# The first key chunk of an adaLN block: key rows in eight loads, the modulation in finer pieces between the key matmuls

## The chip, the cores and the metric

One core of a Trainium2 chip runs the program. The metric is device microseconds (us) of one execution. Five engines matter: TensorE (PE, with its weight loads as PEld), VectorE (DVE), ScalarE (ACT), GpSimd (POOL) and SyncE (SP, which issues nearly all transfers).

## The reference, cut to what matters

```python
x = A_x                                            # 2048 x 1024, bf16
mod = (silu(c) @ w_mod).reshape(1, 6, 1, -1)       # sa, ca, ga, sb, cb, gb: 1024 each
h = layernorm(x) * (1 + ca) + sa
q, k, v = split(h @ wqkv)                          # 32 heads of 32
pq, pk = phi(q), phi(k)                            # where(t > 0, t + 1, exp(t)) + 1e-6
o = (pq @ sum(pk v)) / (pq @ sum(pk) + 1e-6)       # linear attention
x = x + ga * (o @ wo)
h = layernorm(x) * (1 + cb) + sb
out = x + gb * ((silu(h @ w_gate) * (h @ w_up)) @ w_down)
```

## The kernel before, in words

The 2048 rows are cut in four chunks of 512, each of four tiles of 128 rows. A chunk's `hT` holds the layer-normed and modulated rows transposed: 128 columns of the model by 8 blocks `cc` by 512 rows. For the chunks in turn PE computes keys (`k_phase`), values (`v_phase`), queries (`q_phase`) and the sum of key times value (`kv_phase`); after that come the output projection and the gated feed-forward layer, which take most of the time. A key group is a pair (tile `t`, half `nb` of the 1024 key columns); it has an accumulator of 128x512 in one PSUM bank and takes eight matmuls, one for each `cc`.

The change touches only the first key chunk, whose order is written by hand (lines 405 to 450) since everything it needs must first come in. Its parts:

- Loads (lines 114 to 152), all on SP's queue in this order: `c` (2 KB), row tiles 0, 1 and 2 (256 KB each), then for each half b of the columns two modulation blocks `wme` of 1 MB (first those of `ca`, q = 1, then those of `sa`, q = 0) and four of the eight key row blocks `wk` in two loads of 512 KB, with row tile 3 between the halves. After them come the two halves of `wv`, three row tiles of the second chunk, the two halves of `wq`, and more row tiles.
- Row statistics (`ln1_stats`, `bn`, `rstd_of`): two bn_stats, one bn_aggr and an addition on DVE, then the power -0.5 on POOL (`rstd`). For the first chunk `ln1_norm` normalises on DVE (`normalise`); for later chunks POOL makes one more column (`nmr`) and ACT normalises (`normalise_act`), and the transposes are DMAs. In the first chunk PE transposes the eight blocks of a tile into one PSUM bank (`pe_transpose_tile`); ACT copies blocks 0 to 3 to `hT` and DVE blocks 4 to 7.
- `mod_block(b, q)`: 32 matvecs that multiply a block of `w_mod` with silu(c), and a small DVE copy of the four columns to `ca1T` or `saT`. `modulate` on DVE then scales and shifts one block `cc` of `hT` in place.
- `keep_warm(acc, n)`: n matmuls of 128x512 on a tile of zeros, whose result nobody reads; they stand in PE's queue like all others.
- `k_mms` runs key matmuls `cc` by `cc` over a list of groups. Six groups run over tiles 0 to 2, then the two of tile 3 run at the end. `k_evac` computes phi: exp on ACT, min and add on DVE.

PE's instructions stay in the order of the program. `in_order` (line 83) does the same for DVE, ACT and POOL inside the hand-written stretch; what stands outside it (`sc32`, line 449, and `build_masks`, line 450) is put where a scheduler sees room. PSUM has four banks for accumulators of the pool `pa` and four of `pb`; in this stage `pb` holds accumulators, the bank `mod_ps` of the matvecs and the transposes `tp`.

Of the kernel before, what the change touches and what calls it, by code (L numbers as in the profile page):

```python
# [8 lines left out]
ACT = mybir.ActivationFunctionType  # L9
# [12 lines left out]
def kernel(  # L22
# [13 lines left out]
    nc = tc.nc  # L36
    P = nc.NUM_PARTITIONS
    _, S, D = A_x.shape
# [4 lines left out]
    DC = D // P  # L43
    HG = DC
    FC = F // P
    SCW = 512
    NSC = S // SCW
    STC = SCW // P
    NB = 512
# [11 lines left out]
    wqkv_v = A_wqkv.rearrange("(c p) n -> p c n", p=P)  # L61
# [4 lines left out]
    wm_v = w_mod.rearrange("(p j) n -> p j n", j=DC)  # L66
    c_v = c.rearrange("o (p j) -> p (o j)", j=DC)
# [12 lines left out]
    last_on = {}  # L80

    @contextmanager
    def in_order(*engines):
        types = [e.engine for e in engines]
        traced = nc.cur_bb.bb.instructions
        mark = traced[-1]
        yield
        first = next(k for k in reversed(range(len(traced))) if traced[k] is mark) + 1
        for i in traced[first:]:
            if i.engine in types:  # L90
                prev = last_on.get(i.engine)
                if prev is not None:
                    tc.add_manual_dep(i, prev.name, mybir.DependencyInfo(
                        mybir.DependencyClass.NoSync, mybir.DependencyReason.DATA), reason="in_order")
                last_on[i.engine] = i

    def mm(out, lhsT, rhs, start, stop):
        return tc.keep_in_program_order(nc.tensor.matmul(out, lhsT=lhsT, rhs=rhs, start=start, stop=stop))  # L98
# [4 lines left out]
    def big(name, shape):  # L103
        return k8.tile([P] + shape, BF16, name=name, tag="k8")
# [4 lines left out]
    def acc_b(name, shape=(NB,), dt=F32):  # L109
        return pb.tile([P] + list(shape), dt, name=name, tag="pb")  # L110
# [1 line left out]
    x1_dram = dram.tile([S, D], F32, name="x1_scratch")  # L112

    c_sb = const.tile([P, DC], BF16, name="c_sb")
    nc.sync.dma_start(out=c_sb[:], in_=c_v)

    x_tiles = {}

    def load_x(st, eng):
        x_sb = k2.tile([P, D], BF16, name="x_sb")  # L120
        eng.dma_start(out=x_sb[:], in_=x2[st * P:(st + 1) * P, :])
        x_tiles[st] = x_sb

    for st in range(STC - 1):
        load_x(st, nc.sync)

    wme = []
    wk = [big("wk", [4, D]), big("wk", [4, D])]
    for b in range(2):
        ts = []  # L130
        for q in (1, 0):
            t = big("wme", [DC, NB])
            nc.sync.dma_start(out=t[:], in_=wm_v[:, :, q * D + b * NB:q * D + (b + 1) * NB])
            ts.append(t)
        wme.append(ts)
        for i in range(2):
            nc.sync.dma_start(out=wk[b][:, 2 * i:2 * i + 2, :], in_=wqkv_v[:, 4 * b + 2 * i:4 * b + 2 * i + 2, D:2 * D])
        if b == 0:
            load_x(STC - 1, nc.sync)

    def load_w(view, lo, name):
        ts = []
# [14 lines left out]
    nc.vector.memset(neg_half[:], -0.5)  # L157

    scT = const.tile([P, DC], BF16, name="scT")
    nc.scalar.activation(out=scT[:], in_=c_sb[:], func=ACT.Silu)  # L160
    sc32 = const.tile([P, DC, 32], BF16, name="sc32")

    saT = const.tile([P, DC], F32, name="saT")
# [15 lines left out]
    def build_masks():  # L179
        nc.gpsimd.memset(kvmask[:], 0.0)  # L180
        nc.gpsimd.memset(zmask[:], 0.0)
        for h in range(HPC):
            rs = slice(h * DH, (h + 1) * DH)
            nc.gpsimd.memset(kvmask[rs, rs], 1.0)
            for hg in range(HG):
                nc.gpsimd.memset(zmask[rs, hg, HG * h + hg:HG * h + hg + 1], 1.0)  # L186
            nc.gpsimd.memset(sel[h * DH:h * DH + 1, h, :], 1.0)
# [17 lines left out]
    def normalise_act(dst, src, mv, rstd):  # L205
        nmr = small.tile([P, 1], F32, name="nmr")
        nc.gpsimd.tensor_scalar(out=nmr[:], in0=mv[:, 0, 0:1], scalar1=rstd[:, 0:1], scalar2=-1.0,  # L207
                                op0=ALU.mult, op1=ALU.mult)
        nc.scalar.activation(out=dst, in_=src, func=ACT.Identity, bias=nmr[:], scale=rstd[:, 0:1])  # L209

    def modulate(hT, cc, scaleT, biasT, lo=0, hi=SCW):
        nc.vector.tensor_scalar(out=hT[:, cc, lo:hi], in0=hT[:, cc, lo:hi], scalar1=scaleT[:, cc:cc + 1],  # L212
                                scalar2=biasT[:, cc:cc + 1], op0=ALU.mult, op1=ALU.add)

    def pe_transpose_tile(hT, xn, t):
        tp = acc_b("tp", (DC, P), BF16)
        for cc in range(DC):
            transpose(tp[:, cc, :], xn[:, cc * P:(cc + 1) * P])
        h = DC // 2
        nc.scalar.copy(out=hT[:, 0:h, t * P:(t + 1) * P], in_=tp[:, 0:h, :])  # L220
        nc.vector.tensor_copy(out=hT[:, h:DC, t * P:(t + 1) * P], in_=tp[:, h:DC, :])

    hTs = {}

    def ln1_stats(sc, t):
        x_sb = x_tiles.pop(sc * STC + t)
        mv = small.tile([P, STC, 2], F32, name="mv")
        bn(x_sb, mv[:, 0, :])
        rstd = rstd_of(mv, 1)
        return sc, t, x_sb, mv, rstd  # L230

    def ln1_norm(sc, t, x_sb, mv, rstd):
        xn = k2.tile([P, D], BF16, name="xn", bufs=4)
        if sc == 0:
            normalise(xn[:], x_sb[:], mv[:, 0, 0:1], rstd[:, 0:1])
            return xn
        normalise_act(xn[:], x_sb[:], mv, rstd)
        nc.sync.dma_start_transpose(hTs[sc][:, :, t * P:(t + 1) * P], xn[:])

    def ln1(sc):  # L240
        hTs[sc] = big("hT", [DC, SCW])
        for t in range(STC):
            ln1_norm(*ln1_stats(sc, t))

    def mod_block(b, q):
        k = 1 - q
        for i in range(4):
            col = q * DC + 4 * b + i
            for j in range(DC):
                mm(mod_ps[:, col:col + 1], lhsT=wme[b][k][:, j, i * P:(i + 1) * P],  # L250
                   rhs=scT[:, j:j + 1], start=(j == 0), stop=(j == DC - 1))
        cs = slice(4 * b, 4 * b + 4)
        src = mod_ps[:, q * DC + 4 * b:q * DC + 4 * b + 4]
        if q == 1:
            nc.vector.tensor_scalar_add(out=ca1T[:, cs], in0=src, scalar1=1.0)
        else:
            nc.vector.tensor_copy(out=saT[:, cs], in_=src)
# [14 lines left out]
    def k_mms(sc, gs, accs, cc_lo=0, cc_hi=DC):  # L272
        for cc in range(cc_lo, cc_hi):
            for (t, nb), acc in zip(gs, accs):
                mm(acc[:], lhsT=hTs[sc][:, cc, t * P:(t + 1) * P], rhs=wk[cc // 4][:, cc % 4, nb * NB:(nb + 1) * NB],
                   start=(cc == 0), stop=(cc == DC - 1))

    def k_evac(sc, gs, accs):
        for (t, nb), acc in zip(gs, accs):
            phi_to(pks[sc][:, t, nb * NB:(nb + 1) * NB], acc[:])  # L280
# [123 lines left out]
    def keep_warm(acc, n):  # L404
        for _ in range(n):
            mm(acc[:], lhsT=sel[:, 0, :], rhs=sel[:], start=True, stop=True)

    gs = k_groups[0:6]
    accs = [acc_a() if i < 4 else acc_b("acc") for i in range(6)]
    keep_warm(accs[5], 26)  # L410
    hTs[0] = big("hT", [DC, SCW])
    pks[0] = big("pk", [STC, D])
    with in_order(nc.vector, nc.scalar, nc.gpsimd):
        st0 = ln1_stats(0, 0)
        st1 = ln1_stats(0, 1)
        xn0 = ln1_norm(*st0)
        st2 = ln1_stats(0, 2)
        xn1 = ln1_norm(*st1)
        pe_transpose_tile(hTs[0], xn0, 0)
        xn2 = ln1_norm(*st2)  # L420
        keep_warm(accs[5], 4)
        pe_transpose_tile(hTs[0], xn1, 1)
        keep_warm(accs[5], 4)
        pe_transpose_tile(hTs[0], xn2, 2)
        keep_warm(accs[5], 4)
        mod_ps = acc_b("mod_ps")
        for b in range(2):
            idle = accs[5] if b == 0 else accs2[0]
            mod_block(b, 1)
            keep_warm(idle, 2)  # L430
            mod_block(b, 0)
            keep_warm(idle, 3)
            for cc in range(4 * b, 4 * b + 4):
                modulate(hTs[0], cc, ca1T, saT, 0, 3 * P)
            if b == 0:
                xn3 = ln1_norm(*ln1_stats(0, 3))
                k_mms(0, gs, accs, 0, 4)
                pe_transpose_tile(hTs[0], xn3, 3)
                accs2 = [acc_b("acc")]
            else:  # L440
                k_mms(0, gs, accs, 4, 8)
        for cc in range(DC):
            modulate(hTs[0], cc, ca1T, saT, 3 * P, SCW)
        gs2 = k_groups[6:8]
        accs2.append(acc_b("acc"))
        k_mms(0, gs2, accs2)
        k_evac(0, gs, accs)
        k_evac(0, gs2, accs2)
    nc.vector.tensor_copy(out=sc32[:], in_=scT[:].unsqueeze(2).to_broadcast([P, DC, 32]))
    build_masks()  # L450

    for sc in range(NSC):
        if sc > 0:
# [211 lines left out]
```

## Time and profile before

| what | value |
|---|---|
| median of four runs | 845.73 us (845.51 to 846.5) |
| the profiled execution's own time | 845.51 us |
| its span (first to last instruction) | 843.4 us |
| time outside the span | 2.1 us |
| granted TensorE clock over the span | 1.0 |
| read from HBM and written to it | 108.01 MB and 12.71 MB |
| first key matmul starts | 16.30 us |
| first value matmul starts | 33.92 us |

The profile's page has the busy time of each engine, a strip of the span in 40 slices, the chain of work that ended last, and groups of instructions. Answers of the trace used below: the waits of one engine (engine, line, who ended the wait: us in total, times, longest), and a timeline, whose rows are start in us, duration in us, engine, line, operation, output<-inputs, shape and count, with the idle time before the first of them in brackets. A row of several matmuls ends with the last one's end, which is modelled; the next row can start before it. Landing times of transfers are those of the trace.

### The profile page before, as it was taken

What the parts mean: (1) busy time and instruction counts of PE and PEld (TensorE: products, weight loads), DVE (VectorE), ACT (ScalarE), POOL (GpSimd) and SP (SyncE); (2) the same over time, 40 slices, a digit from 0 to 9 for tenths busy, and PEclk for the clock granted to TensorE, in tenths of its full rate; (3) what the DMA queues carried; (4) which work ended last, traced back from release to release, by engine and by line L of the source; (5) the groups of instructions that cost most, each with busy time, mean ns of one, the idle gap of its engine ahead of it and who ended that gap; (6) DMA issues with size and microseconds to landing.
All of it is one profiled execution on the core that took longest, in us unless ns stands there. A gap on an engine that the chain in (4) does not pass through costs nothing.

```text
span 843.4 us, 10565 instructions
## 1 busy us (share of the span) xinstructions
PE 838.0 (99%) x4312; PEld 388.1 (46%) x4312; DVE 307.6 (36%) x604; ACT 173.9 (21%) x267; POOL 55.9 (7%) x160
## 2 busy tenths in 40 slices
PE   9999999999999999999999999999999999999998
PEld 4445445544444444444444444444444444444444
DVE  5747464457433325431112344211114432111122
ACT  1454453363211110101111010011110101111000
POOL 2111010012050001100000010000000100000000
PEclk9999999999999999999999999999999999999999
DMA  9893870029999545528434083581604639720011
GB/s 312 300 264 91 245 188 1 1 52 220 348 243 267 172 150 171 168 69 268 150 100 150 19 237 95 179 261 58 200 1 119 193 69 305 242 71 0 13 63 50
DMA packets 126128, 128.74 MB, mean 153 GB/s; under 512 B 33536, under 2 KB 107776, under 8 KB 125568
## 3 DMA queue, kind: packets, MB, share of 16 engines
q1 hardware_dynamic: 122496, 115.36, 45.6%
q0 software_dynamic: 3584, 12.72, 4.8%
q8 instruction: 33, 0.54, 0.3%
q14 instruction: 15, 0.12, 0.0%
HBM read 108.01 MB, written 12.71 MB: 143 GB/s over the span
## 4 chain that ended last, share of the span: by engine, by line
PE 98%; DVE 1%; POOL 0%; DMA 0%; issue 0%; ACT 0%; SPq 0%; POOLq 0%
PE acc L98 89%; PE a_ps L98 7%; PE kvp L98 1%; PE modr L98 0%; PE wf L98 0%; DMA x_sb<-in_A_x_dram 0%; DVE stats L199 0%; PE mod_ps L98 0%; PE den L98 0%; POOL zmask L186 0%; PE tp L101 0%; POOL rstd L193 0%; PE bcr L98 0%; ACT hT L220 0%; DVE xn L203 0%
## 5 line engine op out<-in xcount | busy, mean ns | idle before, releaser
L98 PE MATMUL acc<-h2T,wgu 128*128 128x512 bf16 x1792 | 387.6, 379 | 0.0
L98 PEld LDWEIGHTS <-wgu 128*128 128x128 bf16 x1792 | 175.3, 98 | 211.3
L98 PE MATMUL acc<-wd,gu 128*128 128x512 bf16 (+2 forms) x924 | 196.1, 373 | 0.0
L572 DVE TENSOR_TENSOR gu<-acc,e 128x512 bf16<-128x512 f32 x112 | 77.4, 692 | 299.3 <-PE acc L98 299.3
L571 ACT ACTIVATE e<-acc 128x512 f32<-128x512 f32 x112 | 67.0, 598 | 374.6 <-PE acc L98 374.6
L98 PEld LDWEIGHTS <-gu 128*128 128x128 bf16 x924 | 89.3, 98 | 104.5
L98 PEld LDWEIGHTS <-hT 128*128 128x128 bf16 x512 | 49.7, 98 | 60.8 <-DVE hT L212 1.0
L593 DVE TENSOR_TENSOR e<-acc,gb_bc 128x512 f32<-128x512 f32 (+2 forms) x33 | 22.3, 675 | 130.0 <-PE acc L98 130.0
L98 PE MATMUL a_ps<-wo,pq 128*128 128x512 bf16 x256 | 57.4, 379 | 0.0
L98 PE MATMUL acc<-hT,wq 128*128 128x512 bf16 x256 | 57.1, 379 | 0.0
L98 PE MATMUL acc<-wk,hT 128*128 128x512 bf16 x256 | 56.9, 379 | 0.0
L98 PE MATMUL acc<-wv,hT 128*128 128x512 bf16 x256 | 55.9, 379 | 0.0
L263 ACT ACTIVATE eb<-acc 128x512 bf16<-128x512 f32 x64 | 37.9, 596 | 62.8 <-PE acc L98 58.2
L209 ACT ACTIVATE xn<-x,nmr,rstd 128x1024 bf16<-128x1024 f32 x16 | 19.8, 1240 | 126.3 <-POOL nmr L207 126.3
L264 DVE TENSOR_SCALAR eb<-eb 128x512 bf16<-128x512 bf16 x64 | 18.3, 290 | 61.0 <-ACT eb L263 61.0
L98 PEld LDWEIGHTS <-pq 128*128 128x128 bf16 x256 | 25.0, 98 | 30.2
L98 PEld LDWEIGHTS <-wq 128*128 128x128 bf16 x256 | 25.0, 98 | 29.8
L540 POOL DMA_DIRECT2D x_scratch<-x x16 | 9.6, 600 | 417.7 <-DVE x L533 417.7
L533 DVE TENSOR_TENSOR x<-a_ps,x_sb 128x512 f32<-128x512 f32 x32 | 22.1, 691 | 8.2 <-PE a_ps L98 8.1
L193 POOL TENSOR_TENSOR rstd<-veps,neg_half 128x1 f32<-128x1 f32 x32 | 18.3, 571 | 82.4 <-DVE veps L191 71.6
L301 ACT CAST v<-acc 128x512 bf16<-128x512 f32 x32 | 18.3, 583 | 22.1 <-PE acc L98 22.1
L596 DVE TENSOR_TENSOR ob<-e,x1r 128x512 bf16<-128x512 f32 (+2 forms) x33 | 22.3, 675 | 1.0
(72 smaller groups left out, 281.3 us busy)
## 6 DMA issues: line engine op xcount, KB each, us to landing
wgu<-in_B_w_gate_dram SPq DMA_DIRECT2D x28, 1024.0 KB, 7.4
wgu<-in_B_w_up_dram SPq DMA_DIRECT2D x28, 1024.0 KB, 8.5
x_sb<-in_A_x_dram SPq DMA_DIRECT2D x32, 256.0 KB, 5.9
wml<-in_w_mod_dram SPq DMA_DIRECT2D x8, 1024.0 KB, 8.9
x_scratch<-x POOLq DMA_DIRECT2D x16, 512.0 KB, 3.3
x1r<-x_scratch SPq DMA_DIRECT2D x31, 256.0 KB, 2.9
wd<-in_B_w_down_dram SPq DMA_DIRECT2D x7, 1024.0 KB, 5.7
wme<-in_w_mod_dram SPq DMA_DIRECT2D x4, 1024.0 KB, 9.9
```

The costliest lines, as they stand in the source:

```text
L98: return tc.keep_in_program_order(nc.tensor.matmul(out, lhsT=lhsT, rhs=rhs, start=start, stop=stop))
L193: nc.gpsimd.tensor_tensor(out=rstd[:, 0:n], in0=veps[:, 0:n], in1=neg_half[:].to_broadcast([P, n]), op=ALU.pow)
L209: nc.scalar.activation(out=dst, in_=src, func=ACT.Identity, bias=nmr[:], scale=rstd[:, 0:1])
L263: nc.scalar.activation(out=e[:], in_=acc, func=ACT.Exp)
L264: nc.vector.tensor_scalar(out=e[:], in0=e[:], scalar1=1.0, scalar2=PHI_EPS, op0=ALU.min, op1=ALU.add)
L301: nc.scalar.copy(out=v[:, t, nb * 4:(nb + 1) * 4, 0:P], in_=acc[:].rearrange("p (g e) -> p g e", e=P))
L533: nc.vector.tensor_tensor(out=x1[:, ns], in0=a_ps[:], in1=x_t[:, ns], op=ALU.add)
L540: nc.gpsimd.dma_start(out=x1_dram[st * P:(st + 1) * P, :], in_=x1[:])
L571: nc.scalar.activation(out=sg[:], in_=ps[0][:], func=ACT.Silu)
L572: gm = nc.vector.tensor_tensor(out=guT[sc][f // GPT][:, f % GPT, :], in0=ps[1][:], in1=sg[:], op=ALU.mult)
L593: nc.vector.tensor_tensor(out=yt, in0=y_ps, in1=gb_bc[:, ns], op=ALU.mult)
L596: nc.vector.tensor_tensor(out=ob, in0=yt, in1=x1r, op=ALU.add)
```

## The change

It moves and cuts the pieces of the first key chunk:

- `c` is loaded after the first three row tiles; silu of it becomes the first instruction of ACT inside the hand-written order.
- The key rows come in eight loads of 256 KB. Row tile 3 is loaded after the first two. The last modulation block (b = 1, q = 0) comes in two halves of 256 columns, with two key row blocks after each.
- The first three tiles are normalised by POOL's `nmr` and ACT, the fourth by DVE. Transposed tiles 0 and 1 are copied by DVE alone, tiles 2 and 3 half and half (now DVE the first half).
- `keep_warm` is called with 20, 1, 1 and 3 in place of 26, 4, 4, 4, 2, 3, 2 and 3.
- `mod_block` takes a range of its four columns. The blocks of `sa` are done in two halves, each followed by its copy and two `modulate`s. The second pair of blocks stands between key matmuls: `ca`'s after the fourth `cc`, then four matmuls of group 7, then the first half of `sa`'s, and the other half in the middle of `cc` = 5.
- Group 7 runs with the six from `cc` = 4 on, group 8 runs alone at the end.
- `sc32` and `build_masks` are issued after the last DVE and POOL instruction of the stretch.

In the built program, the rest of PE's instructions keep their order. On SP one more row tile of the second chunk stands ahead of `wq`, and each load waits, as before, for the landing of the one issued eight before it on that queue.

```diff
 for st in range(STC - 1):
     load_x(st, nc.sync)
-wme = []
+nc.sync.dma_start(out=c_sb[:], in_=c_v)
 wk = [big("wk", [4, D]), big("wk", [4, D])]
-for b in range(2):
-    ts = []
-    for q in (1, 0):
-        t = big("wme", [DC, NB])
-        nc.sync.dma_start(out=t[:], in_=wm_v[:, :, q * D + b * NB:q * D + (b + 1) * NB])
-        ts.append(t)
-    wme.append(ts)
-    for i in range(2):
-        nc.sync.dma_start(out=wk[b][:, 2 * i:2 * i + 2, :], in_=wqkv_v[:, 4 * b + 2 * i:4 * b + 2 * i + 2, D:2 * D])
-    if b == 0:
-        load_x(STC - 1, nc.sync)
+wme = [[big("wme", [DC, NB]) for _ in range(2)] for _ in range(2)]
+def load_mod(b, q, lo, hi):
+    nc.sync.dma_start(out=wme[b][q][:, :, lo:hi], in_=wm_v[:, :, q * D + b * NB + lo:q * D + b * NB + hi])
+def load_k(cc):
+    nc.sync.dma_start(out=wk[cc // 4][:, cc % 4, :], in_=wqkv_v[:, cc, D:2 * D])
+load_mod(0, 1, 0, NB)
+load_mod(0, 0, 0, NB)
+load_k(0)
+load_k(1)
+load_x(STC - 1, nc.sync)
+load_k(2)
+load_k(3)
+load_mod(1, 1, 0, NB)
+load_mod(1, 0, 0, NB // 2)
+load_k(4)
+load_k(5)
+load_mod(1, 0, NB // 2, NB)
+load_k(6)
+load_k(7)
...
-def pe_transpose_tile(hT, xn, t):
+def pe_transpose_tile(hT, xn, t, split):
...
-    h = DC // 2
-    nc.scalar.copy(out=hT[:, 0:h, t * P:(t + 1) * P], in_=tp[:, 0:h, :])
-    nc.vector.tensor_copy(out=hT[:, h:DC, t * P:(t + 1) * P], in_=tp[:, h:DC, :])
+    if split < DC:
+        nc.scalar.copy(out=hT[:, split:DC, t * P:(t + 1) * P], in_=tp[:, split:DC, :])
+    nc.vector.tensor_copy(out=hT[:, 0:split, t * P:(t + 1) * P], in_=tp[:, 0:split, :])
...
-def ln1_norm(sc, t, x_sb, mv, rstd):
+def ln1_norm(sc, t, x_sb, mv, rstd, dve=False):
     xn = k2.tile([P, D], BF16, name="xn", bufs=4)
-    if sc == 0:
+    if dve:
         normalise(xn[:], x_sb[:], mv[:, 0, 0:1], rstd[:, 0:1])
-        return xn
-    normalise_act(xn[:], x_sb[:], mv, rstd)
+    else:
+        normalise_act(xn[:], x_sb[:], mv, rstd)
...
-keep_warm(accs[5], 26)
+spare = accs[5]
+keep_warm(spare, 20)
...
 with in_order(nc.vector, nc.scalar, nc.gpsimd):
+    nc.scalar.activation(out=scT[:], in_=c_sb[:], func=ACT.Silu)
+    xns = [ln1_norm(*ln1_stats(0, t)) for t in range(3)]
+    mod_ps = acc_b("mod_ps")
+    pe_transpose_tile(hT, xns[0], 0, DC)
+    keep_warm(spare, 1)
+    mod_block(0, 1, 0, 4)
+    pe_transpose_tile(hT, xns[1], 1, DC)
+    keep_warm(spare, 1)
+    pe_transpose_tile(hT, xns[2], 2, DC // 2)
+    keep_warm(spare, 3)
+    mod_block(0, 0, 0, 2)
+    for cc in (0, 1):
+        modulate(hT, cc, ca1T, saT, 0, H)
+    mod_block(0, 0, 2, 4)
+    for cc in (2, 3):
+        modulate(hT, cc, ca1T, saT, 0, H)
+    k_mms(0, gs, accs, 0, 3)
+    xn3 = ln1_norm(*ln1_stats(0, 3), dve=True)
+    pe_transpose_tile(hT, xn3, 3, DC // 2)
+    k_mms(0, gs, accs, 3, 4)
+    for cc in range(4):
+        modulate(hT, cc, ca1T, saT, H, SCW)
+    mod_block(1, 1, 0, 4)
+    gs7, accs7 = k_groups[6:7], [acc_b("acc")]
+    k_mms(0, gs7, accs7, 0, 4)
+    mod_block(1, 0, 0, 2)
+    for cc in (4, 5):
+        modulate(hT, cc, ca1T, saT)
+    k_mms(0, gs + gs7, accs + accs7, 4, 5)
+    k_mms(0, gs[0:4], accs[0:4], 5, 6)
+    mod_block(1, 0, 2, 4)
+    for cc in (6, 7):
+        modulate(hT, cc, ca1T, saT)
+    k_mms(0, gs[4:6] + gs7, accs[4:6] + accs7, 5, 6)
+    k_mms(0, gs + gs7, accs + accs7, 6, 8)
+    gs8, accs8 = k_groups[7:8], [acc_b("acc")]
+    k_mms(0, gs8, accs8)
...
-nc.vector.tensor_copy(out=sc32[:], in_=scT[:].unsqueeze(2).to_broadcast([P, DC, 32]))
-build_masks()
+with tc.issue_after(last_on[nc.vector.engine]):
+    nc.vector.tensor_copy(out=sc32[:], in_=scT[:].unsqueeze(2).to_broadcast([P, DC, 32]))
+with tc.issue_after(last_on[nc.gpsimd.engine]):
+    build_masks()
```

More of the change, by code (lines that the diff above doesn't have):

```diff
@@ L114 @@
     c_sb = const.tile([P, DC], BF16, name="c_sb")
-    nc.sync.dma_start(out=c_sb[:], in_=c_v)
     x_tiles = {}
@@ L159 @@
     scT = const.tile([P, DC], BF16, name="scT")
-    nc.scalar.activation(out=scT[:], in_=c_sb[:], func=ACT.Silu)
     sc32 = const.tile([P, DC, 32], BF16, name="sc32")
@@ L230, in ln1_stats @@
         return sc, t, x_sb, mv, rstd
-    def ln1_norm(sc, t, x_sb, mv, rstd):
+    def ln1_norm(sc, t, x_sb, mv, rstd, dve=False):
         xn = k2.tile([P, D], BF16, name="xn", bufs=4)
-        if sc == 0:
+        if dve:
             normalise(xn[:], x_sb[:], mv[:, 0, 0:1], rstd[:, 0:1])
-            return xn
-        normalise_act(xn[:], x_sb[:], mv, rstd)
-        nc.sync.dma_start_transpose(hTs[sc][:, :, t * P:(t + 1) * P], xn[:])
+        else:
+            normalise_act(xn[:], x_sb[:], mv, rstd)
+        if sc > 0:
+            nc.sync.dma_start_transpose(hTs[sc][:, :, t * P:(t + 1) * P], xn[:])
+        return xn
     def ln1(sc):
@@ L243, in ln1, with mod_block @@
             ln1_norm(*ln1_stats(sc, t))
-    def mod_block(b, q):
-        k = 1 - q
-        for i in range(4):
+    def mod_block(b, q, lo, hi):
+        for i in range(lo, hi):
             col = q * DC + 4 * b + i
             for j in range(DC):
-                mm(mod_ps[:, col:col + 1], lhsT=wme[b][k][:, j, i * P:(i + 1) * P],
+                mm(mod_ps[:, col:col + 1], lhsT=wme[b][q][:, j, i * P:(i + 1) * P],
                    rhs=scT[:, j:j + 1], start=(j == 0), stop=(j == DC - 1))
-        cs = slice(4 * b, 4 * b + 4)
-        src = mod_ps[:, q * DC + 4 * b:q * DC + 4 * b + 4]
+        cs = slice(4 * b + lo, 4 * b + hi)
+        src = mod_ps[:, q * DC + 4 * b + lo:q * DC + 4 * b + hi]
         if q == 1:
@@ L409 @@
     accs = [acc_a() if i < 4 else acc_b("acc") for i in range(6)]
-    keep_warm(accs[5], 26)
-    hTs[0] = big("hT", [DC, SCW])
+    spare = accs[5]
+    keep_warm(spare, 20)
+    hT = hTs[0] = big("hT", [DC, SCW])
     pks[0] = big("pk", [STC, D])
+    H = 3 * P
     with in_order(nc.vector, nc.scalar, nc.gpsimd):
[L414 to L425, printed above, removed]
-        mod_ps = acc_b("mod_ps")
[L427 to L446, printed above, removed]
-        k_evac(0, gs, accs)
-        k_evac(0, gs2, accs2)
@@ L452 @@
+        k_mms(0, gs8, accs8)
+        k_evac(0, gs, accs)
+        k_evac(0, gs7, accs7)
+        k_evac(0, gs8, accs8)
+    with tc.issue_after(last_on[nc.vector.engine]):
+        nc.vector.tensor_copy(out=sc32[:], in_=scT[:].unsqueeze(2).to_broadcast([P, DC, 32]))
+    with tc.issue_after(last_on[nc.gpsimd.engine]):
+        build_masks()
     for sc in range(NSC):
```

## The prediction, on record before the result

> **What bounds the kernel now.** I read the page's engine table first, then the waits of TensorE (PE) alone, then PE's timeline over the first 75 us.
>
> ```profile
> span 843.4 us, 10565 instructions
> PE 838.0 (99%) x4312; PEld 388.1 (46%) x4312; DVE 307.6 (36%) x604; ACT 173.9 (21%) x267; POOL 55.9 (7%) x160
> ```
>
> PE is busy 838.0 of 843.4 us. The missing 5.4 us can be named: the last matmul ends at 840.06, so 3.34 us are the tail after PE; the rest is all of PE's waits:
>
> ```profile
> PE acc L98 <- DVE sel L402: 1.2, 1, 1.2
> PE tp L101 <- DVE xn L203: 0.5, 1, 0.5
> PE acc L98 <- DVE hT L221: 0.4, 1, 0.4
> ```
>
> All three lie before 24 us. From there to the end PE never waits, so an edit in the first stage is worth exactly what it takes from PE's stream there: matmuls taken out, plus waits taken out, minus waits put in. The stream itself:
>
> ```profile
> 1.21 7.83 PE L98 MATMUL acc<-sel 128*128 128x512 bf16 x26 [1.21 <-DVE sel L402]
> 8.87 0.61 PE L101 MATMUL tp<-ident,xn 128*128 128x128 bf16 x8
> ...
> 12.14 0.62 PE L101 MATMUL tp<-ident,xn 128*128 128x128 bf16 x8 [0.48 <-DVE xn L203]
> ...
> 16.30 5.35 PE L98 MATMUL acc<-wk,hT 128*128 128x512 bf16 x24
> 21.50 0.61 PE L101 MATMUL tp<-ident,xn 128*128 128x128 bf16 x8
> 21.94 0.94 PE L98 MATMUL mod_ps<-scT,wme 128*128 128x1 bf16 x32
> 23.24 0.59 PE L98 MATMUL acc<-sel 128*128 128x512 bf16 x2 [0.35 <-DVE hT L221]
> 23.67 0.94 PE L98 MATMUL mod_ps<-scT,wme 128*128 128x1 bf16 x32
> 24.47 0.81 PE L98 MATMUL acc<-sel 128*128 128x512 bf16 x3
> 25.28 8.81 PE L98 MATMUL acc<-wk,hT 128*128 128x512 bf16 x40
> 33.92 13.98 PE L98 MATMUL acc<-wv,hT 128*128 128x512 bf16 x64
> ```
>
> The `acc<-sel` rows are the filling: 26+12+5+5 = 48 matmuls whose result nobody reads. The reader is to see that PE is full because it is filled, and that V begins at 33.92 right behind the last key matmul. Transfers are near but not late. The trace's landings: row tiles 0 to 2 at 4.04, 4.73, 5.41; the first two modulation blocks 9.16 and 12.23; the key rows 13.58 and 14.93; row tile 3 15.65; modulation 18.59 and 22.38; key rows 23.73 and 25.09; the two V halves 27.81 and 30.46. Each was there before its first reader.
>
> **The change, part by part.**
>
> *Filling out.* 48 become 20+1+1+3 = 25. In the trace they start 427 ns apart up to 5.02, and 216 ns apart from 5.42 on; the 23 dropped are of the later kind: 23 x 0.216 = 4.97 us out. The old waits of 0.48 and 0.35 go with the stretches that held them: 5.8 us can be won at most. What is late next decides how much stays.
>
> *Rows at the front.* The load of c goes behind three row tiles, so these issue one slot of 0.46 us earlier: tile 0 lands at 3.58. On DVE a tile then takes 1.63 us (from the start of its stats at 5.77: 7.48 for the end of veps, the next stats could start at 7.40). Veps end at 5.32, 6.95 and 8.58. The normalising moves from DVE (0.55) to ACT, in the form of the second chunk: rstd 0.55, nmr 0.27 and ACTIVATE 1.24 run from veps' end at 40.49 to 42.77, so 2.28 us. xn is ready at 7.60, 9.23 and 10.86, where it was 7.94, 10.10 and 12.09. The third wins most: its rstd stood 1.4 us behind mask memsets on POOL (veps done 9.56, rstd at 10.95). The masks now come after the fourth tile's rstd; POOL was idle for 13.9 us before 40.57, so that costs nothing, nor does the copy of sc32 (0.28 us) at the end of the stage.
>
> *A new head of ACT's queue.* Silu of c now stands ahead of the three normalisings and waits for c. c issued at 2.12 lands no earlier than the old 1.64 us after issue (3.8) and no later than the block issued behind it (9.16); I take 5.1, just behind row tile 2 at 4.95, whose bytes it follows. Silu (0.21) is done before nmr needs ACT at 6.36. At 9.16 the normalisings would end 3 us later.
>
> *Evacuation.* Tiles 0 and 1 are copied by DVE alone. 128x1024 is not in the trace: between one 128x512 (0.42) and two (0.85); I take 0.8, as it is twice the elements. It hides: tile 0's copy runs to about 9.4, before tile 2's transposes need that bank.
>
> *PE up to the first key matmul.* 20 fillings end at about 7.6 (the 20th starts at 7.36). Transposes of tile 0 with xn0: 7.66 to 8.1; one filling, 8.3; then the first modulation block: its load issues in the same slot as before, its bytes follow rows that are 0.46 earlier, so 8.7 to 9.16; I take 9.1: **wait 0.75**. 32 matvecs 0.8 (rows at 13.46 and 14.26): 9.9. Tile 1 and a filling to 10.55; tile 2 waits for xn2 until 10.9: **wait 0.3**. With three fillings 12.0; the second block lands 11.8 to 12.23: **wait 0.2**. Its matvecs come in two halves, and in the built program the second half waits for DVE's copy of the first (saT, 0.16, plus some 0.1 of hand-over): **wait 0.3**, bounded by 0 and by 0.6 (the 0.35 and 0.48 rows are the nearest). Key matmul one: about 13.45, against 16.30.
>
> *From there to V.* 18 key matmuls (0.2165 each) to 17.35. Tile 3 arrives earlier (its load now stands before the third and fourth key rows: 14.1), DVE is free at 14.4, and stats to xn took 2.92 (17.04 to 19.96): 17.3, **no wait to 0.2**. Transposes 0.45, six key matmuls, 32 matvecs: 19.95; four matmuls of the seventh group 20.8. The next half block: landings repeat the old pace (0.68 per 256 KB, 2.94 for the whole block), 18.5 for the block before it. Packets of 512 B are not in the trace; those of 256 B took 22 ns and of 1024 B 50 ns, so 64 per engine make 1.4 to 3.2 us a half; I take 2.0, near the middle, as time goes with size from 256 up to 2048 B (90 ns). Landing 20.5 and, with two key rows between, 23.9: hidden. Then the matvecs' result must pass DVE before key matmuls go on, with no filling over it: last matvec to copy to modulate (0.33 for 128x512, row of the second chunk) : **wait 0.8**. 11 key matmuls to 24.5, 16 matvecs 0.4, three matmuls that cover the same DVE chain: **wait 0.1**. 14 + 8 matmuls: V starts at about 30.6.
>
> *V's loads.* V needs its second half with its fifth matmul, at 31.5; that landed at 30.46 and moves by the two halves' extra (some 0.6) to about 31. Hidden by half a us; this caps the whole gain at about 4. Bank 0 is free (first group complete by 27.4, exp, min and add 1.6 us).
>
> *Eight key loads.* The old K waited for no key load, so finer loads remove no wait. Their rate: 256 KB row tiles landed 0.69 us apart (380 GB/s), 512 KB key loads 1.35 (388). I cost the split at nothing; the cover is V's half us.
> On SP each load waits, as before, for the landing of the one eight before it: the last key row for the third (14.8), the first V half for the fourth (15.5), long before their turn at 24 and 26.
> The Trainium skill, page "DMA: Bandwidth & Descriptors", section "Bandwidth", asks for 1 MiB a DMA, and the section "Anatomy of one DMA" puts 2.0 us of fixed time in each (measured for loads issued from GpSimd; these go from SP). Were that paid in series, four more key loads would cost 8 us and the sum would be about 850; landings 0.69 us apart in this trace speak for overlap.
>
> *Sum.* V before: last key matmul's stream ends at 33.70; after: 30.6. Gain **3.1 us**. The ledger agrees: 4.97 + 0.83 out, 0.1+0.75+0.3+0.2+0.3+0.1+0.8+0.1 = 2.65 in, gives 3.15. Behind V the order of PE is the same and nothing waits. The second chunk's transposes had landed by 52.92 and are read at 59.86; one more row tile ahead of wq puts wq at 38.5, read from 44.6. The profiled run was 845.51 (span 843.4 + 2.1); median of the four 845.73. Forecast 845.51 - 3.1 = **842.4**.
>
> **Rivals.** *Late transfers.* If 512 B packets cost like 1024 B ones (3.2 a half), the last half and everything behind it lands 2.4 later; the second half's matvecs then start at 26.3 instead of 24.5: 844.2. Against: 256 B packets are at 22 ns.
>
> *Silu blocks ACT.* If c lands only with the block behind it, xn2 comes at about 13.9, not 10.86, and K at 15.6: 844.6. For: it is queued behind 768 KB. Against: it is queued before the block.
>
> *The clock (ends slower).* Place: 7.6 to 13.5 and 19 to 25, where filling goes and PE stands or does one-column matvecs for about half the time. Each key matmul at 427 instead of 216 ns costs 0.21. Full rate came 4.2 us after PE's start; one loss of it, regained after 4.2 us of work, costs 2.1: 844.5. Two bring 846.6. From 15 slow key matmuls the gain is gone; if the clock stays low for the whole K stage, 64 x 0.21 = 13.5: 856. Against: a gap of 0.48 changed nothing, and at the end the clock fell only at 845.05, 5 us after the last matmul.
> The Trainium skill, page "TensorE: Matmul & The Clock Gate", has two rules that differ: under "HAM oscillation" only idle gaps above about 3.4 us count, which leaves 842.4; under "A second HAM failure mode" short idles between groups suffice, which gives 844.5 to 846.6.
>
> *Not what it says.* Key loads in eight may do nothing, and the filling's removal all: the time is then the same 842.4, with key matmuls that wait for DVE and never for wk.
>
> **How the numbers follow.** Forecast 0.76 (841.4 by V's cap to 843.6 with every wait at its upper bound); late transfers 0.06; Silu 0.03; clock lost once or twice 0.09; held low for the stage 0.06. What differs by under 0.2% (1.7 us) can't be told from no change: faster 0.76, same 0.06+0.03+0.09 = 0.18, slower 0.06. Range 841.2 to 844.7: it takes in the cases at 844.2 to 844.6 and leaves out the clock lost twice or held, and some tail.
>
> **What would show it.** First key matmul at 13.45 and V at 30.6 in PE's timeline; PE waits of about 2.7 us in place of 0.83; key matmuls 216 ns apart throughout; xn2 ready at 10.9. Wrong if the clock falls, if PE waits for wk or wv, or if PE waits again behind V.

## The result, and the profile after

The changed kernel takes 843.59 us (median of 35 runs, 842.23 to 846.25) against 845.7 (55 runs of the kernel before); the ratio is 0.9974, 95% interval 0.9970 to 0.9979. That is 2.2 us less by the ratio, clear of no change; 3.1 had been forecast, and the time lies inside the range.

The 35 timed runs and the profiled one are of two kinds, and the granted TensorE clock, which is recorded for every run, parts them. In 20 of 36 it averaged at least 0.9985 over the span (below: full), and their median is 843.1. In 16 it was 0.996 to 0.998 (below: lost); their median is 844.75. The profiled run, 844.92, is one of those. Lines of its page:

```profile
span 842.8 us, 10528 instructions
PE 835.6 (99%) x4289; PEld 386.8 (46%) x4289; DVE 306.7 (36%) x599; ACT 176.3 (21%) x268; POOL 55.8 (7%) x163
```

PE's count is down by exactly the 23 fillings, and its busy time by only 2.4 us where 4.97 went out. All its waits, from the waits of PE:

```profile
PE mod_ps L98 <- DMA wme<-in_w_mod_dram: 1.3, 1, 1.3
PE acc L98 <- DVE sel L412: 1.2, 1, 1.2
PE acc L98 <- DVE hT L221: 0.7, 1, 0.7
PE tp L101 <- ACT xn L218: 0.3, 1, 0.3
PE mod_ps L98 <- DVE saT L267: 0.2, 1, 0.2
```

Without the first 1.2, which is older than the change, that is 2.5 us of waiting; 2.65 had been forecast. So waiting does not explain the missing part. PE's timeline does:

```profile
1.21 6.11 PE L98 MATMUL acc<-sel 128*128 128x512 bf16 x20 [1.21 <-DVE sel L412]
7.57 0.62 PE L101 MATMUL tp<-ident,xn 128*128 128x128 bf16 x8 [0.26 <-ACT xn L218]
8.03 0.38 PE L98 MATMUL acc<-sel 128*128 128x512 bf16 x1
9.67 0.95 PE L98 MATMUL mod_ps<-scT,wme 128*128 128x1 bf16 x32 [1.26 <-DMA wme<-in_w_mod_dram]
10.48 0.61 PE L101 MATMUL tp<-ident,xn 128*128 128x128 bf16 x8
10.93 0.38 PE L98 MATMUL acc<-sel 128*128 128x512 bf16 x1
11.14 0.87 PE L101 MATMUL tp<-ident,xn 128*128 128x128 bf16 x8
11.80 1.49 PE L98 MATMUL acc<-sel 128*128 128x512 bf16 x3
...
14.37 5.91 PE L98 MATMUL acc<-wk,hT 128*128 128x512 bf16 x18
...
33.16 13.98 PE L98 MATMUL acc<-wv,hT 128*128 128x512 bf16 x64
```

Two rows of eight transposes stand one above the other: 0.61 us at 10.48, 0.87 at 11.14. Three fillings take 1.49 where at full rate they take 0.81. The first key matmul starts at 14.37, not 13.45; its 18 take 5.91 where 18 x 0.2165 plus the last one's drain make 4.1. The clock fell in the middle of this, as the windows of the trace show. Columns: stretch and length; busy time and count of PE, PEld, DVE, ACT, POOL; granted clock; DMA share; GB/s.

```profile
4.51:7.92 3.41, 3.15 (x20) 1.43 (x19) 3.27 (x9) 1.47 (x3) 1.64 (x4) 1.00 0.96 309
7.92:11.34 3.42, 2.16 (x51) 1.71 (x49) 1.47 (x6) 2.46 (x2) 0.82 (x2) 1.00 0.99 301
11.34:14.75 3.41, 3.16 (x44) 2.02 (x42) 1.85 (x7) 0.59 (x1) 0.00 (x0) 0.50 1.06 397
14.75:18.16 3.41, 3.41 (x9) 1.18 (x8) 2.67 (x7) 0.00 (x0) 1.04 (x5) 0.50 1.10 347
18.16:21.58 3.42, 3.42 (x23) 1.82 (x22) 0.44 (x2) 0.80 (x2) 2.40 (x40) 1.00 1.14 330
```

The clock is 1.00, then 0.50 for 6.83 us, then 1.00 to the end. The edges of these windows are not chosen: the record has the clock change at 4.51, 11.34 and 18.16, and I cut between them in halves. In the stretch before the fall PE is busy 2.16 of 3.42 us, and 0.8 of that are matvecs of one column. Twelve wide matmuls (three fillings, nine key matmuls) ran at 427 ns, 0.21 us more each: 2.5 us. Not all of it reaches the end of the run, since part of it lies over the landing of the second block (12.57, read at 13.08): the median of the lost runs is 1.65 us above that of the full ones. The one trace of the changed kernel is of a lost run; whether late landings and lost clocks come together in its runs, so that the 1.65 is not the clock's alone, no run separates.

V starts at 33.16, 0.76 before the old 33.92, and the span is 0.6 shorter: what is won at V's start is nearly all there at the end. From V's start to the end of the last matmul PE takes 806.14 us in both traces.

### The profile page after: what moved, and what is told of

It is laid out like the page before. It is cut to its first block, busy times and chain, and to the rows that moved or that the text cites. A ratio compares the mean times of both kernels' runs of the same rounds, so it can differ in the third digit from the quotient of the medians.

```text
span 842.8 us, 10528 instructions
## 1 busy us (share of the span) xinstructions
PE 835.6 (99%) x4289; PEld 386.8 (46%) x4289; DVE 306.7 (36%) x599; ACT 176.3 (21%) x268; POOL 55.8 (7%) x163
## 4 chain that ended last, share of the span: by engine, by line
PE 98%; DMA 1%; SPq 0%; DVE 0%; issue 0%
PE acc L98 89%; PE a_ps L98 7%; PE kvp L98 1%; DMA wme<-in_w_mod_dram 1%; PE modr L98 0%; PE mod_ps L98 0%; PE wf L98 0%; PE tp L101 0%; PE den L98 0%; SPq L120 0%; PE bcr L98 0%; SPq L125 0%; DVE hT L221 0%; PE mcol L98 0%; DVE saT L267 0%
## 5 line engine op out<-in xcount | busy, mean ns | idle before, releaser
L98 PE MATMUL acc<-wk,hT 128*128 128x512 bf16 x256 | 59.4, 388 | 0.7 <-DVE hT L221 0.7
```

## The experiments

Theory after the result: the gain is the filling that was taken out, less the waits beneath, and in some runs the clock is lost because the stage became too empty. Rivals: late transfers take the missing part; the reordering or the filling alone makes the gain. Numbers: median of all runs, ratio to the kernel before with its interval, and in how many runs the clock stayed full.

| kernel | fillings | median us | ratio (95%) | clock full |
|---|---|---|---|---|
| after | 25 | 843.59 | 0.9974 (0.9970 to 0.9979) | 20 of 36 |
| e1_fill | 30 | 843.61 | 0.9976 (0.9967 to 0.9986) | 9 of 10 |
| e3_nofill | 20 | 845.42 | 0.9993 (0.9984 to 1.0002) | 0 of 11 |
| e6_oldfill | 43 | 845.50 | 0.9995 (0.9986 to 1.0004) | 11 of 11 |
| e4_before_thin | 25 | 848.77 | 1.0040 (1.0027 to 1.0052) | 0 of 5 |
| e12_matvecs | 25 | 843.23 | 0.9973 (0.9964 to 0.9983) | 8 of 10 |
| e2_pairs | 25 | 844.73 | 0.9984 (0.9975 to 0.9992) | 4 of 11 |
| e5_whole | 25 | 844.68 | 0.9990 (0.9981 to 0.9999) | 5 of 12 |
| e8_x3early | 30 | 845.33 | 0.9995 (0.9986 to 1.0003) | 5 of 11 |
| e7_cover | 30 | 843.33 | 0.9971 (0.9961 to 0.9981) | 8 of 8 |
| e9_rows | 30 | 843.08 | 0.9972 (0.9962 to 0.9982) | 6 of 9 |
| e10_halves | 33 | 844.42 | 0.9978 (0.9970 to 0.9987) | 11 of 11 |
| e11_halves2 | 33 | 844.15 | 0.9975 (0.9963 to 0.9987) | 6 of 12 |

The runs of the kernel before beside these had a full clock in 98 of 109, with a median of 845.5 (845.5 to 845.6 in each of the five groups that ran together); the other 11 have a median of 847.65, so the old filling did not always keep the clock either. No trace shows such a run.

**e1_fill: the gap filled.**

```diff
 pe_transpose_tile(hT, xns[0], 0, DC)
-keep_warm(spare, 1)
+keep_warm(spare, 6)
```

> After, with six fillings instead of one between the transposes of tile 0 and the first modulation block, where PE stood for 1.26 us. Theory (in half of the runs the granted clock falls for 6.8 us because this stretch is too empty; 5 more matmuls of 0.216 lie inside the wait): granted clock 1.0 in nearly all runs, median 842.7 to 843.2, spread under 1.2 us. Rival (the missing microsecond comes from late transfers, and the clock falls whatever stands there): median 843.6 or more, the runs as far apart as before (842.2 to 846.3), clock below 0.9985 in some half of them.

The clock was full in 9 of 10 runs, as the theory has it; the rival's half did not come. The time expected did not come either: the median is 843.6, not 842.7 to 843.2, and the runs lie 2.2 us apart, not 1.2. So the filling keeps the clock, and what that should win is not seen in the median. The same stretches in its trace, from the first full clock on:

```profile
6.32:9.73 3.41, 3.41 (x23) 1.71 (x21) 2.80 (x8) 2.61 (x3) 1.63 (x4) 1.00 1.03 346
9.73:13.15 3.42, 2.89 (x52) 2.00 (x52) 1.23 (x3) 1.69 (x2) 0.00 (x0) 1.00 1.04 352
...
```

The full clock came at 6.32 here, at 4.51 in after's trace, between 3.90 and 7.19 in all of them: the stretches lie differently over the same work in every run, which fits one kernel's having both kinds of run.

Why the median gains nothing is shown in part. In this trace the five fillings delay nothing: the first block landed at 9.99 and was read at 10.04. The second landed at 13.45, and PE waited 0.73 us for it. And here PE does lose time behind V, in a later chunk's keys; e1_fill first, then the changed kernel:

```profile
120.38 2.67 DVE L221 TENSOR_SCALAR hT<-hT,ca1T,saT 128x512 bf16<-128x512 bf16 x8 [2.21 <-DMA hT<-xn]
121.10 4.13 PE L98 MATMUL acc<-wk,hT 128*128 128x512 bf16 x16
```

```profile
119.87 2.67 DVE L221 TENSOR_SCALAR hT<-hT,ca1T,saT 128x512 bf16<-128x512 bf16 x8 [0.92 <-DMA hT<-xn]
122.48 3.62 PE L98 MATMUL acc<-wk,hT 128*128 128x512 bf16 x16
```

PE now comes 0.7 us behind DVE, not 2.6, and follows it from one modulated block to the next at 0.32 us a matmul. From V's start to the last matmul it takes 806.65 us instead of 806.14, and the list of waits does not show it, as each piece is only 0.1 us. The same stands in the traces of e6_oldfill, e7_cover, e8_x3early and e9_rows (806.45 to 806.77), and in no other.

**e3_nofill: the small fillings out.**

```diff
-keep_warm(spare, 1)    # after tile 0
-keep_warm(spare, 1)    # after tile 1
-keep_warm(spare, 3)    # after tile 2
```

> After, without the five small fillings (1, 1 and 3) between the first transposes and matvecs. Theory of the clock: 5 x 0.216 = 1.1 us come out of PE's stream but most of it only becomes waiting for the modulation blocks; the clock falls in most runs, median 844.5 to 845. Rival (PE's stream alone counts, the clock does not depend on it): 842.5 to 843.6, the clock as in the changed kernel.

The clock was lost in all 11 runs and the time is 845.4, a little above what was expected. What was taken out came back as waiting (2.5 us for the blocks where after has 1.3, in one trace each) and at half clock.

**e6_oldfill: the new order with nearly the old filling.**

```diff
-keep_warm(spare, 20)
+keep_warm(spare, 26)
...
-keep_warm(spare, 1)    # tiles 0 and 1
+keep_warm(spare, 4)
...
-keep_warm(spare, 3)
+keep_warm(spare, 9)
```

> After, with 26, 4, 4 and 9 fillings in its four places instead of 20, 1, 1 and 3: 18 more. Theory (the gain is filling taken out, less what then becomes waiting): 18 x 0.216 = 3.9 us in, of which the waits of 0.3 and 1.3 us and some 0.5 of the second block swallow about 2: first key matmul near 15.5, 845.0 to 845.6, clock 1.0. Rival (the new order of rows, matvecs and key matmuls makes the gain, the filling does not matter): 843 to 843.6.

845.5, no gain left, as the theory has it; the first key matmul stands at 16.31, where it stood before, and not near 15.5. In its trace V starts at 33.43, 0.5 before the old 33.92, and the 0.6 lost behind V takes that back. The new order beneath the filling shows no gain.

**e4_before_thin: the old order with the new filling.**

```diff
-keep_warm(accs[5], 26)
+keep_warm(accs[5], 20)
...
-keep_warm(accs[5], 4)  # three times
+keep_warm(accs[5], 1)  # 1, 1 and 3
...
-keep_warm(idle, 2)
...
-keep_warm(idle, 3)
```

> The kernel before, with its filling cut to 20, 1, 1, 3, and none around the matvecs: 23 fewer, nothing else changed. Theory (filling was cover for waits, the reorder shortens the waits beneath): the third row tile (12.09) then holds the start, first key matmul near 14.9, one more us won behind: 843.4 to 844.2 with a full clock, 1 to 2 us more in runs in which it falls. Rival (cutting the filling is all that the change does): 842.5 to 843.2, at or below the changed kernel.

Both expectations fell: it is slower than the kernel before. Its trace shows where to:

```profile
PE tp L101 <- DVE xn L203: 2.1, 2, 1.1
PE acc L98 <- DVE hT L212: 1.3, 2, 0.7
PE acc L98 <- DVE sel L402: 1.2, 1, 1.2
PE mod_ps L98 <- DVE ca1T L255: 0.7, 2, 0.4
...
```

4.1 us of waiting for DVE stand where the kernel before had 0.83, so 3.3 of the 4.97 taken out came back as waits, and the clock is lost twice (0.5 from 17.28 to 20.69 and from 27.52 to 30.93). In the old order the filling was cover for DVE, and beneath it are waits two thirds as long. By these rows alone 1.7 us would be won; it is the clock, lost twice and in this trace not full before 7.04, that makes the kernel slower. No run of it had a full clock, so the 843.4 to 844.2 expected for one was not tested. Neither half of the change gains alone: the order with nearly all the filling 0.9995, the cut without the order 1.0040, both 0.9974.

**e12_matvecs: what counts for the clock.**

```diff
 keep_warm(spare, 1)
+for _ in range(48):
+    mm(spare[:, 0:1], lhsT=sel[:, 0, :], rhs=sel[:, 0, 0:1], start=True, stop=True)
```

> After, with 48 matvecs of one column (25 ns each, 1.2 us) instead of the five more fillings in the gap before the first modulation block; nobody reads them. In the traces so far the clock fell behind stretches of 3.41 us with at most 1.17 us of wide matmuls in them, matvecs not counted. Theory (the clock goes by the array's work, and one-column matvecs hardly count): PE looks busy in the gap, yet the clock is lost in a third or more of the runs, median 843.5 to 845. Rival (it goes by PE standing still): clock full in all or nearly all runs, as with six fillings, median 843.0 to 843.7.

Lost in 2 of 10 runs: neither a third nor none, and with ten runs not to be told from e1_fill's 1 of 10, nor from after's 16 of 36. Whether matvecs count is not shown by it.

To see what does, I cut all 14 traces (the kernel before included) from their first full clock into stretches of 3.413 us, the step in which the clock's records lie, up to about 34 us, and took the rate at which matmuls start: 0.216 us for one of 512 columns, 0.056 for one of 128 (both called wide here), 0.025 for a matvec. In eleven traces single matmuls have no record; they show as two starts 0.43 us apart with next to no idle time between, and are counted in. Six falls are in the traces. The six stretches before them held 0.45 to 1.29 us of wide matmuls (plus 0.5 to 1.2 of matvecs). The emptiest that passed at full clock held 1.35, 1.37 and 1.38 (each plus 1.2 of matvecs); one passed with 1.41 and no matvec at all. So a fall stands behind a stretch of 3.41 us in which wide matmuls fill less than about two fifths, and matvecs need no part in it: counted with 0.14 of their time or less they leave this order as it is, with more they upset it. That the clock goes by the time PE stands still, the rival, does not fit the stretch without a matvec, in e10_halves:

```profile
16.87:20.28 3.41, 1.59 (x9) 0.63 (x9) 2.49 (x6) 0.00 (x0) 1.46 (x8) 1.00 1.14 336
```

PE is busy 1.59 of 3.41 us there, with a gap of 1.82, and the clock stays; five of the six falls came behind stretches in which it was busy 2.05 to 2.44. All this is read from 14 traces, the fullest stretch before a fall (1.29) and the emptiest that passed (1.35) lie only 0.06 us apart, and the bound was not tested by itself.

**e2_pairs: the key rows in four loads.**

```diff
-    nc.sync.dma_start(out=wk[cc // 4][:, cc % 4, :], in_=wqkv_v[:, cc, D:2 * D])
+    nc.sync.dma_start(out=wk[cc // 4][:, cc % 4:cc % 4 + 2, :], in_=wqkv_v[:, cc:cc + 2, D:2 * D])
...
-load_k(1)    # and 3, 5, 7
```

> After, with the eight key rows in four loads of 512 KB (rows 0-1, 2-3, 4-5, 6-7, in the same places). Theory (the split of the key rows does nothing, since PE waits for no key load): same as after within 0.5 us, clock lost in about half the runs, no wait of PE for wk. Rival (the finer loads are what lets the key matmuls start): a wait for wk at the first key matmul of up to 0.7 us, 844.2 or more.

PE waits for no key load in its trace; runs with a full clock have 842.4 to 843.6 (four runs), no worse than after's 843.1. The median of all, 844.73, is more than the 0.5 us above after's that was allowed for; it comes from 7 lost clocks in 11, against 16 in 36, which chance can give. The eight loads do nothing that these runs show.

**e5_whole: the last block in one load.**

```diff
-load_mod(1, 0, 0, NB // 2)
+load_mod(1, 0, 0, NB)
 load_k(4)
 load_k(5)
-load_mod(1, 0, NB // 2, NB)
```

> After, with the last modulation block in one load of 1 MB ahead of key rows 4 to 7. Theory (the halves pay: the first half's matvecs stood at 23.5, the whole block lands some 1.5 us after its first half): PE waits for it 0.5 to 1.2 us more, 844.0 to 844.8. Rival (packets of 512 B cost more than they bring): the later loads land 0.3 to 0.6 earlier and the time is 843.0 to 843.6.

With a full clock 843.75 (five runs), 0.65 more than after; in its trace PE waits for the block 0.42 us:

```profile
22.11 0.55 PE L98 MATMUL mod_ps<-scT,wme 128*128 128x1 bf16 x16 [0.42 <-DMA wme<-in_w_mod_dram]
```

By these two numbers the halves pay about half a microsecond; five runs, from 842.89 to 844.15, don't fix it closer. 512 B packets took 32 ns each in after's trace, a half 1.7 to 1.8 us.

**e8_x3early: 256 KB more ahead of the second block** (on e1_fill).

```diff
+load_x(STC - 1, nc.sync)
 load_mod(0, 0, 0, NB)
 load_k(0)
 load_k(1)
-load_x(STC - 1, nc.sync)
```

> The kernel with six fillings, and row tile 3 loaded before the second modulation block instead of behind two key rows: 256 KB or 0.68 us more stand before that block. Theory (the landing of the second modulation block sets the first key matmul, in place of the rows and the filling): first key matmul 0.5 to 0.7 later, 844.1 to 844.4. Rival (PE's own stream or the rows set it): unchanged, 843.6.

With a full clock 844.39 (five runs) against e1_fill's 843.6: 0.8 us for 0.68 us of load. In both traces PE waits for the second block right before the first key matmuls (0.72 and 0.73 us), so its landing sets them. The two traces do not show the 0.68 itself: the block landed at 13.60 here and at 13.45 there, as landings vary between runs. The clock was lost in 6 of 11 runs, against 1 of 10 with the same 30 fillings; that the added wait does it fits, and so few runs do not prove it.

**e7_cover: the four matmuls of group 7 over DVE's chain** (on e1_fill).

```diff
-k_mms(0, gs7, accs7, 0, 4)
 mod_block(1, 0, 0, 2)
 for cc in (4, 5):
     modulate(hT, cc, ca1T, saT)
+k_mms(0, gs7, accs7, 0, 4)
```

> The kernel with six fillings, and in it the first half of the last modulation block ahead of the four matmuls of group 7 instead of behind them, so that these 0.86 us lie over the 0.70 that PE waits for DVE before the fifth column block. Theory: that wait goes, the half block's landing (21.5) may cost 0.25: 0.4 to 0.7 us less than the kernel with six fillings, so 842.9 to 843.2. Rival (V waits for its own loads anyway): 843.6, with a wait of PE for wv.

```profile
...
PE mod_ps L98 <- DVE hT L230: 0.5, 1, 0.5
PE mod_ps L98 <- DVE ca1T L265: 0.3, 1, 0.3
PE mod_ps L98 <- DVE saT L267: 0.2, 1, 0.2
...
```

The wait of 0.7 for the modulated `hT` (L221) is gone, 0.3 for `ca1T` came; the 0.5 put down to `hT` (L230), the copy of a transposed tile, is more likely the second block, which landed 0.04 us before that wait ended (in e9_rows the same matvecs start before that copy ends). 843.33, with no lost clock in 8 runs: 0.3 below e1_fill where 0.4 to 0.7 was expected, and not to be told from it. In this run the first block landed at 10.70, later than in any other trace, and 0.4 us went behind V.

**e9_rows: the row part undone** (on e7_cover): the first three tiles normalised by DVE in the old order, masks and `sc32` free again.

```diff
-xns = [ln1_norm(*ln1_stats(0, t)) for t in range(3)]
+st0 = ln1_stats(0, 0)
+st1 = ln1_stats(0, 1)
+xns = [ln1_norm(*st0, dve=True)]
+st2 = ln1_stats(0, 2)
+xns += [ln1_norm(*st1, dve=True), ln1_norm(*st2, dve=True)]
...
-with tc.issue_after(last_on[nc.vector.engine]):
-    nc.vector.tensor_copy(out=sc32[:], in_=scT[:].unsqueeze(2).to_broadcast([P, DC, 32]))
-with tc.issue_after(last_on[nc.gpsimd.engine]):
-    build_masks()
+nc.vector.tensor_copy(out=sc32[:], in_=scT[:].unsqueeze(2).to_broadcast([P, DC, 32]))
+build_masks()
```

> The kernel with six fillings and the cover for the half block (e7_cover), with the row part of the change undone: the first three tiles normalised by DVE in the old order, the masks and sc32 again where the scheduler puts them. Theory (the second modulation block, landing at 12.6 to 13.9, sets the first key matmul, so rows that are 1.2 us later are still in time): third xn near 12.0, no loss above 0.4 us against e7_cover, so 843.2 to 843.8, clock full or nearly. Rival (the row part carries its share of the gain): 844.3 or more.

843.08, no loss. In its trace PE stands 0.87 us before tile 2's transposes and reads the second block at 12.75; the block landed at 12.27, so about half of the 0.87 would have been waited for anyway, and all of it where that block lands at 13 or later. The row part shows no gain here. The clock was lost in 3 of 9 runs, against none of 8, which chance can give.

**e10_halves and e11_halves2: attempts to go further** (on e7_cover).

```diff
-load_mod(0, 0, 0, NB)
+load_mod(0, 0, 0, NB // 2)
 load_k(0)
 load_k(1)
+load_mod(0, 0, NB // 2, NB)    # e11: behind row tile 3
...
+keep_warm(spare, 3)
+st3 = ln1_stats(0, 3)          # e11 only; e10 has it behind the second modulates
+k_mms(0, gs, accs, 0, 1)
+k_mms(0, gs[0:3], accs[0:3], 1, 2)
 mod_block(0, 0, 2, 4)
 for cc in (2, 3):
     modulate(hT, cc, ca1T, saT, 0, H)
-k_mms(0, gs, accs, 0, 3)
+k_mms(0, gs[3:6], accs[3:6], 1, 2)
+k_mms(0, gs, accs, 2, 3)
```

In both, V of the first chunk runs its first four groups over column blocks 0 to 3 and then over 4 to 7.

> e7_cover, with the second modulation block also loaded in halves (its first 256 columns, two key rows, the rest), the second half's matvecs in the middle of the second column block, three fillings over DVE's chain before the first key matmul, and in the first chunk's V the first four groups run over the first four column blocks before the second V half is needed. Theory (landings at the front and then the second V half are what is left): first key matmul near 13.5, V about 0.5 us earlier than in e7_cover, 842.5 to 843.0. Rival (512 B packets and the fuller queue give it back further on): 843.3 or more, with waits for wk or wv.

The first key matmul came at 13.71, but DVE reached tile 3's statistics later, and PE stood 1.82 us before its transposes; with the clock full in all 11 runs the median is 844.42, not 842.5 to 843.0:

```profile
20.16 0.62 PE L101 MATMUL tp<-ident,xn 128*128 128x128 bf16 x8 [1.82 <-DVE xn L213]
```

> e10_halves, in which PE stood 1.8 us before tile 3's transposes because its statistics came behind the second half's modulation on DVE: row tile 3 is now loaded before that half block, and its statistics stand before that half's copy. Theory: this wait goes, V starts near 31.0, clock full: 842.3 to 842.9, below the changed kernel in every run with a lost clock and by 0.3 to 1.0 us in the median. Rival (the time comes back as a wait for the half block, for wk or for the second V half): 843.5 or more, with that wait in PE's list.

That wait went and the key matmuls started at 13.25; now PE was early for the next blocks (waits of 0.20 and 0.83), as the rival has it, and the clock fell there:

```profile
18.98:22.40 3.42, 2.39 (x54) 1.57 (x53) 1.57 (x6) 1.56 (x2) 0.00 (x0) 1.00 1.14 330
22.40:25.81 3.41, 3.41 (x12) 1.22 (x10) 0.89 (x3) 0.00 (x0) 0.00 (x0) 0.50 1.09 358
25.81:29.22 3.41, 3.38 (x31) 1.56 (x30) 0.89 (x3) 0.00 (x0) 0.00 (x0) 1.00 1.05 384
```

With a full clock it has 842.9 (six runs), the others 845.2. No kernel tried is told from the changed one as faster; e7_cover is level with it and kept its clock in all of its 8 runs.

## Why the prediction was right or wrong

- **The ledger of PE held in the trace.** That PE's stream is the time, that an edit in the stage is worth matmuls and waits out less waits in, and that nothing behind V gives it back: 23 matmuls fewer, 2.5 us of waits against 2.65, 806.14 us from V to the last matmul in both traces. Runs with a full clock gained 2.4 us (845.5, beside the experiments, to 843.1), 0.7 short of the forecast. Of its signs, the waits and xn2 (10.76 for 10.9) came. The first key matmul (14.37 for 13.45), V (33.16 for 30.6) and 216 ns throughout did not, and a falling clock was named there as a sign of being wrong. With a full clock, e1_fill, e5_whole and e12_matvecs have the first key matmul at 13.9 to 14.7 and V at 31.5 to 31.8.
- **That nothing gives it back behind V** is not so for every kernel near this one: five of the experiments' traces lose 0.3 to 0.6 us at a later chunk's keys. The one trace of the changed kernel does not; of its other runs this is not known.
- **One reading is off.** 33.70 is where the last key matmul starts; its stream ends where V starts, at 33.92. By the two places the gain is then 3.3, by the ledger 3.15; the forecast took 3.1.
- **The single waits differ.** The first block: 1.26 for 0.75. xn of tile 2: none for 0.3, since PE was late itself (ready at 10.76; forecast 10.86). The `saT` hand-over 0.25 for 0.3; DVE's chain 0.70 for 0.8; the first transposes 0.26 for 0.1; none for the second block's 0.2, as PE came to it late, at half clock, nor for the last two of 0.1. That the sum agrees so well, 2.5 for 2.65, is luck.
- **The landings were too early by half a microsecond and too certain.** The forecast had the first two blocks at 9.1 and 12.0, from one trace. After's has 9.62 and 12.57, and the other kernels that load as it does had 8.9 to 10.7 and 12.3 to 13.9. The kernel before read its second block at 14.69 and did not feel this; the changed one reads it on arrival. The waits for it in e1_fill and e8_x3early show that this landing is what counts. That is 0.5 of the 0.7; the rest is not traced.
- **The step that failed is the clock.** It stood as a rival with 0.09 for "lost once or twice" and a price of 2.1 us, 844.5. It was lost in 16 of 36 runs, so the chance was far too low. The lost runs' median of 844.75 is close to the 844.5 by luck: the price measured is 1.65, not 2.1 (which it is between the two kinds of run of the kernel before), on top of a full-clock time that is 0.7 above the forecast. The argument against it, "a gap of 0.48 changed nothing", looked at single gaps; by the stretches above it is what the array does over 3.41 us that orders the falls. The median of 843.59 lies between the two kinds of run, and where it falls hangs on how many of each there are: that it lies inside the range says little for the mechanism.
- **The Trainium skill's two rules, weighed there, part here.** Of the page "TensorE: Matmul & The Clock Gate", the rule under "HAM oscillation" (no idle gap above about 3.4 us) would have kept the clock: the longest gap was 1.26 us, and it fell. The one under "A second HAM failure mode" (short idles between groups suffice), which the page gives for a kernel that cycles PSUM banks, agrees in kind: in e11_halves2 the clock fell with no gap above 0.83 us in the stretch before. The window of 3413 ns that the page gives under "Part 1" agrees with the records: stretches of half clock lasted 3.41 or 6.83 us.
- **Late transfers** came in part, by another way: not the 512 B packets (1.7 to 1.8 us a half, 2.0 taken), but the big blocks. **Silu** was right: c landed at 5.25 (5.1), silu was done at 5.48, and xn came at 7.51, 9.14 and 10.76.
- **"Not what it says"** was right for the eight key loads (e2_pairs), and also for the row part (e9_rows), to which the forecast had given a share. The rival's other half, that the filling's removal makes it all, is not borne out: without the new order the kernel is 0.4% slower, with the clock lost in all five runs (e4_before_thin).

## What to carry to other kernels

Filling that keeps an engine busy is often cover for a wait: before it is cut, work out the wait beneath, and cut only after the work has been moved so that the wait is gone. On TensorE it has a second use: add up the wide matmuls over every stretch of 3.4 us, wherever such a stretch may begin, and keep well above two fifths (here stretches with 1.29 us or less were followed by a fall, those with 1.35 or more were not). Time taken out of a kernel that waited for nothing is won only up to the next thing that is merely a little early, and how early that is varies from run to run: one trace's landing time is not a bound. And look for it along the whole run, start to start, as a list of waits leaves out what is lost in pieces of 0.1 us.

## What the runs showed of the hardware that was not expected

- The clock fell to 0.5, for 3.41 or 6.83 us, behind stretches of 3.41 us with 0.45 to 1.29 us of wide matmuls. In e11_halves2 no gap of PE in that stretch was above 0.83 us; in e10_halves a gap of 1.82, in a stretch with 1.41, did not bring it down.
- The first full clock came 2.7 to 6.0 us after PE's first matmul (3.90 to 7.19 in fourteen traces), in no relation to the kernel that shows.
- The first modulation block, 1 MB issued at 2.6 in each of the kernels with the changed loads, landed between 8.66 and 10.70.
- 128x1024 from PSUM took DVE 0.68 us, less than two copies of 128x512 (0.42 each).
